# Two layers' attention over one key/value cache: small work, pieces and weights re-timed around the change of layer

## Chip, cores and metric

The kernel runs on one core of one Trainium2 chip. The metric is the device time of one execution in microseconds (us). Engines are named as in the profile: PE (matrix products), DVE (vector work), ACT (activations), POOL, and SP, whose queue issues nearly all DMA transfers.

## What is computed

Two rounds of the same pair of blocks, with one query row per batch, 32 query heads on 8 cache heads, 32768 cached rows of 128 numbers, 2 batches, float32. The shapes that matter: `k_cache` and `v_cache` are (2, 8, 32768, 128), some 537 MB each, and both layers read the same caches and the same weights.

```python
def _A_ref(x, k_cache, v_cache, wq, wo):          # x: (2, 1, 512)
    q = heads(x @ wq)                              # 32 heads of 128
    scores = q . k * (128 ** -0.5)                 # 4 query heads share a cache head
    o = softmax(scores) . v
    return o @ wo                                  # (2, 1, 512)
def _B_ref(x, w1, b1, w2, b2):                     # mixer over one token, 1792 hidden
    h = _layernorm(x)
    return sum_f(_gelu(h * w1 + b1) * w2) + b2
x = x + _A_ref(_layernorm(x), ...)
x = x + _B_ref(_layernorm(x), ...)
x = x + _A_ref(_layernorm(x), ...)
x = x + _B_ref(_layernorm(x), ...)
```

The second layer's query of a batch needs the first layer's whole result for that batch, mixer included.

## The kernel before

**Units and steps.** A unit is (layer, batch, head). Its K and its V are 64 cells each; a cell is 128 partitions x 512 float32, 0.262 MB. `Order` (L41 to L110) writes the sequence by hand as steps of 4 cells (`STEP`): 16 K steps (`k_step`, L328, products at L335), later 16 V steps (`v_step`, L379, products at L388). In the ordinary part K of one unit alternates with V of the unit before. Between K and V of a unit lie its maximum (`max_1`, `max_2`), the transposes (L365) and the exponentials on ACT (L370).

**The two changes of layer** (`changes`, L65). For batch 0, x = (0,0,7) is the last unit of layer 0, y = (1,0,7) the first of layer 1, and fill = (0,1,6) a unit of the other batch put between; for batch 1 they are (0,1,7), (1,1,7) and (1,0,6). x and y use the same cache head, so the first 10 cells of K (`KEPT_K`) and all 64 of V (`KEPT_V`) stay in memory from x to y and are not loaded again. The order is K(x), [V before], K(fill), V(x), V(fill), K(y), V(y) and so on. While the 16 steps of V(fill) run, the mixer of the batch is worked through in hooks after them: hidden tiles on ACT (L527), their products (L511), then `change_0` to `change_3` (L565 to L594), which make the new layer's query row by row. K(y) starts in the step after V(fill).

**Hooks.** `at(p, f, ...)` puts small work behind step p in program order (L705 to L803). Each engine runs its own instructions in that order, so a small product stands in PE's queue between two steps. For a unit these are among others `denominators` (L407: a sum on DVE, a small product L411, a reciprocal L413), `take_out` (L417: the accumulator copied to the tile `row`, of which there is one), `out_1` (products L427, then L442) and `out_2` (products with the output weights, L451). The `us=` of a hook is what the planner is told of its cost. `unread` (L599) issues products whose result nobody reads, on PE alone; one of width G is a product of 512 columns (two PE records, L605).

**Memory and loads.** `mem` holds 106 cells. `plan_loads` (L113) lays out, ahead of time, every transfer: it goes through the steps in order, chooses for each run of missing cells a size (of `SIZES`, 32 down to 4 cells, or the size that `order.sizes` fixes by `cut`, L97) and a place with the least forecast wait, and the step after which the transfer may be issued, that is, after which the last user of that place is done. All these transfers go out in this one order on SP's queue (L823, weights L816); an issue that has to wait for PE holds all later ones. While y's K streams, 64 cells hold the kept V and 16 the weights of heads 6 and 7, which both layers share; 26 are left, 10 of them with the kept K until those steps are done.

**Sizes around the change.** V(fill) goes in 16 pieces of 4 cells. Of K(y), cells 10 and 11 come as one piece of 2; the rest is left to the planner, which made pieces of 4 up to cell 39 and then 8, 8, 8 for the first change, and pieces of 4 up to cell 47 and then 8, 8 for the second.

**Weights.** wq and wo of a head are one transfer of 8 cells. It is asked for 24 steps ahead of the head's first K step (L737), and the query products (`make_q`, L284; products L300) stand 10, 8 and 6 steps ahead of it (L732). Six weights belong to layer 1 alone (heads 5 to 0); that of head 5 comes right behind K of the second y.

Of the kernel before, what the change touches and what calls it, by code (L numbers as in the profile page):

```python
# [14 lines left out]
G = 512  # L15
HALF = 32
STEP = 4
# [4 lines left out]
KEPT_K = 10  # L22
# [18 lines left out]
class Order:  # L41


    def __init__(self, heads):
        far, f, s = list(range(heads - 2)), heads - 2, heads - 1
        self.steps = []
        self.pairs = []
        before = [(0, b, h) for h in far for b in (0, 1)] + [(0, 0, f)]
        x0, fill0, y0 = (0, 0, s), (0, 1, f), (1, 0, s)
        x1, fill1, y1, n = (0, 1, s), (1, 0, f), (1, 1, s), (1, 1, f)  # L50
        after = [(1, b, h) for h in far[:1:-1] for b in (0, 1)] + [(1, b, h) for b in (0, 1) for h in far[1::-1]]
        for i, u in enumerate(before):
            self.k(u)
            if i:
                self.v(before[i - 1])
        self.k(x0), self.v(before[-1]), self.k(fill0), self.v(x0), self.v(fill0)
        self.k(y0), self.v(y0), self.k(x1), self.k(fill1), self.v(x1), self.v(fill1)
        self.k(y1), self.v(y1), self.k(n)
        prev = n
        for u in after:  # L60
            self.k(u), self.v(prev)
            prev = u
        self.v(prev)
        self.last = prev
        self.changes = ((x0, fill0, y0), (x1, fill1, y1))  # L65
        self.units = before + [x0, fill0, y0, x1, fill1, y1, n] + after
        self.first, self.end = {}, {}
        for p, (kind, u, g) in enumerate(self.steps):
            self.first.setdefault((kind, u), p)
            self.end[kind, u, g // HALF] = p  # L70
        byv = sorted(self.units, key=lambda u: self.first["V", u])
        self.v_before = {u: byv[i - 1] if i else None for i, u in enumerate(byv)}
        self.last_of = {
            (layer, b): max((u for u in self.units if u[:2] == (layer, b)), key=lambda u: self.end["V", u, 1])
            for layer in (0, 1)
            for b in (0, 1)
        }
        self.first_of = {
            (layer, b): min((u for u in self.units if u[:2] == (layer, b)), key=lambda u: self.end["V", u, 1])
            for layer in (0, 1)  # L80
            for b in (0, 1)
        }
        self.kept = {}
        for x, _, y in self.changes:
            for g in range(KEPT_K):
                self.kept["K", x, g] = ("K", y, g)
            for g in range(KEPT_V):
                self.kept["V", x, g] = ("V", y, g)
        self.sizes = {}
        for x, fill, y in self.changes:  # L90
            self.cut("K", y, KEPT_K, (-KEPT_K % STEP,))
            self.cut("V", x, HALF, TAPER)
            self.cut("V", fill, 0, (STEP,) * 16)
        self.cut("V", self.last, 0, (HALF // 2, HALF // 2))
        self.cut("V", self.last, HALF, FINAL)
# [100 lines left out]
def gqa_mixer_kernel(ctx: ExitStack, tc: tile.TileContext, x, kt, v, wqo, cols, out):  # L196
# [10 lines left out]
    order = Order(HKV)  # L207
    steps, first, end = order.steps, order.first, order.end
# [498 lines left out]
    def at(p, f, *args, us=0.0):  # L707
        hooks.setdefault(p, []).append((f, args))
        busy[p] = busy.get(p, 0.0) + us
# [6 lines left out]
    changed = {y: (x, fill) for x, fill, y in order.changes}  # L716
    opening = order.units[0]
    weights, made = [], {opening}
    users = {}
    for u in order.units:  # L720
        layer, b, h = u
        users.setdefault(h if h >= HKV - 2 else (layer, h), []).append(u)
        k0 = first["K", u]
# [3 lines left out]
        us = (u, mate) if b == 0 and mate not in made and (layer == 0 or h < HKV - 2) else (u,)  # L727
# [5 lines left out]
    for name, us in users.items():  # L733
        k0 = min(first["K", u] for u in us)
        h = name if isinstance(name, int) else name[1]
        layer = min(u[0] for u in us)
        weights.append((k0 - 24 if k0 else -1, (layer, h), max(end["V", u, 1] for u in us) + 3))  # L737

    for u in order.units:
        layer, b, h = u  # L740
        key = (layer, b)
        k_mid, k_end = end["K", u, 0], end["K", u, 1]
        v0, v_mid, v_end = first["V", u], end["V", u, 0], end["V", u, 1]
        ahead = order.v_before[u]
        p1, p2 = (k_end + 2, k_end + 4) if k_end + 4 < v0 else (k_end, k_end)
        t0 = max(k_mid, end["V", ahead, 0] if ahead else 0)
        t1 = max(k_end, end["V", ahead, 1] if ahead else 0)
        if p2 <= t0:
            at(p1, max_1, u, us=0.2), at(p2, max_2, u, us=0.2)
            at(t0, turn_scores, u, 0), at(t0, exponentials, u, 0)  # L750
        else:
            at(t0, turn_scores, u, 0)
            at(p1, max_1, u, us=0.2), at(p2, max_2, u, us=0.2)
            at(p2, exponentials, u, 0, us=5.0 if p1 == p2 else 0.0)
        at(t1, turn_scores, u, 1)
        at(max(t1, p2), exponentials, u, 1)
        at(v0 - 1 if u == order.last else v_mid + 2, denominators, u, us=0.4)
        if u == order.last:
            at(v0 - 1, take_rows, key)
            at(v0 - 1, table, AF.Gelu_apprx_tanh)  # L760
            at(v0 - 1, mix_1, key)
            at(v0 - 1, last_rows, u)
            at(v_mid, unread, u, G, 3)
            at(v_mid + 4, unread, u, P, 2)
            at(v_end - 2, take_out, u)
            at(v_end - 2, unread, u, G)
            at(v_end - 1, out_sum, u)
            at(v_end, last_mixer, u)
            continue
        at(v_end, take_out, u)  # L770
        if u != order.last_of[key]:
            late = 0 if u == order.v_before[order.last] else 1
            at(v_end + late, out_1, u, us=1.2)
            at(v_end + 2 * late, out_2, u, us=2.0)
            continue
        e = v_end
        at(e - 2, mix_1, key, us=1.2)
        at(e, out_1, u, us=1.9)
        at(e + 1, out_2, u, us=2.0)
        at(e + 1, take_rows, key)  # L780
        at(e + 2, mix_2, key, us=1.2)
        if layer == 0:
            at(e + 2, unread, u, G // 2)
            at(e + 3, half_way, key, us=1.0)
            at(e + 3, unread, u, G)
        at(e + 2, table, AF.Gelu_apprx_tanh)
        for k in range(FT // 2 + 1):
            at(e + 3 + k, hidden_tiles, key, k, us=0.7 if k else 0.0)
        e += 3 + FT // 2
        at(e, take_rows, key)  # L790
        at(e, table, AF.Exp)
        if layer == 1:
            at(e + 1, mix_4, key, us=1.2)
            continue
        (y,) = [y for y, (x, _) in changed.items() if x == u]
        at(e + 1, change_0, key, us=1.0)
        at(e + 1, unread, u, G // 2)
        at(e + 2, change_1, key, y, us=1.2)
        at(e + 3, change_2, key, y, us=0.4)
        at(e + 3, unread, u, G)  # L800
        at(e + 4, change_3, y, us=1.0)
        at(e + 4, unread, u, G // 2)
        assert e + 4 < first["K", y]  # L803

    loads = plan_loads(order, weights, busy)
    finals = [a for label, s, a, _ in loads if label[:2] == ("V", order.last)]
# [83 lines left out]
```

## Time and profile before

| what | value |
|---|---|
| median of 3 runs | 2507.3 us (2506.25 to 2511.06) |
| the profiled execution's own time | 2505.95 us |
| its span in the profile, first to last instruction | 2504.1 us |
| mean granted PE clock | 0.757 of full |
| bytes that SP's queue moved | 1064.32 MB |

The view by windows, which the prediction quotes, gives, for stretches of the span (start:end in us, then the length), the busy time of each engine with its number of instructions, the granted PE clock (1.00 is full, 0.50 half), the mean busy share of the 16 DMA engines, and the GB/s moved. A row of the timeline gives the start and duration, the engine and line, what is read and written, the number of instructions merged, and in brackets how long the engine stood idle before and what ended that.

### The profile page before, as it was taken

To read this page: it belongs to the slowest core of one execution; us is meant where nothing else is said; L and a number is where in the kernel's file an instruction comes from. 1 tells how busy PE (TensorE), PEld (TensorE's weight loads), DVE (VectorE), ACT (ScalarE), POOL (GpSimd) and SP (SyncE) were. 2 spreads that over 40 slices of the span, in tenths; PEclk is the share of its full clock that TensorE was granted. 3 is DMA by queue.
4 is the path that set the end of the run, shared out by engine and by line. 5 is a ranking of instruction groups with operands and counts; after the bars stand their busy time and mean duration, and the time that the engine had idled before them with its cause. 6 is when DMAs were issued, how large, how long until landed. Compare 5 with 4: busy or idle time off the path is not lost. (4 is left out here: it accounts for less than half of the span.)

```text
span 2504.1 us, 21186 instructions
## 1 busy us (share of the span) xinstructions
PE 1383.1 (55%) x9682; PEld 395.9 (16%) x9682; DVE 180.3 (7%) x487; ACT 185.8 (7%) x579; POOL 5.1 (0%) x18
## 2 busy tenths in 40 slices
PE   3455555554455554556776774455465545555567
PEld 1111111111111111111121121111111111111112
DVE  1000000000000000001010010000000000000012
ACT  0100000000000000001110101000000000000021
POOL 0000000000000000000000000000000000000000
PEclk9777776777767767778788887777777777677788
DMA  9999999999999999999999999999999999999996
GB/s 418 431 428 433 436 429 434 436 430 431 432 433 434 433 433 430 416 431 420 409 423 426 414 415 442 432 429 434 431 435 434 429 429 438 429 433 434 428 432 284
DMA packets 33075, 1065.70 MB, mean 426 GB/s; under 512 B 3925, under 2 KB 3929, under 8 KB 5082
## 3 DMA queue, kind: packets, MB, share of 16 engines
q1 hardware_dynamic: 32696, 1064.32, 99.0%
q8 instruction: 76, 1.25, 0.2%
q14 instruction: 13, 0.11, 0.0%
q10 hardware_dynamic: 290, 0.03, 0.0%
HBM read 1064.33 MB, written 0.00 MB: 425 GB/s over the span
## 5 line engine op out<-in xcount | busy, mean ns | idle before, releaser
L335 PE MATMUL scores<-mem,qz 128*32 128x512 f32 x4096 | 605.3, 734 | 549.5 <-DMA mem<-in_kt_dram 549.5
L388 PE MATMUL acc<-mem,S 128*16 128x512 f32 x4080 | 593.2, 714 | 539.7 <-DMA mem<-in_v_dram 534.7
L370 ACT ACTIVATE S<-S,neg 128x128 f32<-128x128 f32 x256 | 129.7, 509 | 2240.9 <-DVE S L365 1205.6
L335 PEld LDWEIGHTS scores<-mem,qz 128*32 128x32 f32 x4096 | 136.4, 128 | 951.1 <-issue 476.2
L388 PEld LDWEIGHTS acc<-mem,S 128*16 128x16 f32 x4080 | 125.1, 107 | 857.2 <-issue 776.6
L345 DVE TENSOR_REDUCE mx<-scores 128x1 f32<-128x512 f32 x64 | 44.2, 691 | 839.5 <-PE scores L335 831.7
L427 PEld LDWEIGHTS misc<-selg,row 128*128 128x128 f32 x256 | 48.9, 285 | 48.2 <-issue 36.8
L365 DVE STREAM_TRANSPOSE S<-scores 128x512 f32<-128x512 f32 x64 | 45.4, 710 | 118.9 <-PE acc L388 118.9
L427 PE MATMUL misc<-selg,row 128*128 128x4 f32 x256 | 51.7, 325 | 3.3 <-DVE row L419 3.2
L451 PE MATMUL rows<-mem,oT 128*1 128x512 f32 x248 | 51.0, 912 | 0.3 <-DVE oT L442 0.3
L370 ACT ACTIVATION_READ_ACCUMULATOR S<-S,neg 128x1 f32 x256 | 47.7, 186 | 0.0
L355 DVE TENSOR_REDUCE m<-misc 1x4 f32<-1x128 f32 x32 | 8.9, 279 | 357.7 <-PE misc L353 357.7
L419 DVE COPY row<-acc 128x512 f32<-128x512 f32 x32 | 22.1, 691 | 173.5 <-PE acc L388 173.5
L413 DVE RECIPROCAL rl<-misc 128x4 f32<-128x4 f32 x32 | 5.8, 182 | 343.3 <-PE misc L411 343.3
L442 DVE TENSOR_TENSOR oT<-misc,rl 128x4 f32<-128x4 f32 x32 | 5.2, 162 | 273.1 <-PE misc L427 272.6
L411 PEld LDWEIGHTS misc<-both,one 128*128 128x128 f32 x64 | 14.1, 275 | 51.7 <-issue 45.7
L300 PE MATMUL misc<-mem,xw 128*32 128x512 f32 x144 | 20.9, 641 | 1.9 <-DVE xw L276 1.9
L307 PEld LDWEIGHTS misc<-selg,row 128*128 128x128 f32 x128 | 16.3, 199 | 17.7 <-issue 8.4
L411 PE MATMUL misc<-both,one 128*128 128x4 f32 x64 | 16.8, 333 | 4.1 <-DVE both L410 4.1
L527 ACT ACTIVATE row<-bcast,bias,scale 128x512 f32<-128x512 f32 x21 | 16.3, 777 | 29.8 <-PE rows L511 16.2
L307 PE MATMUL misc<-selg,row 128*128 128x2 f32 (+1 forms) x128 | 17.7, 260 | 0.8 <-DVE row L292 0.8
L353 PE MATMUL misc<-ident,mxa 128*1 128x128 f32 x64 | 16.7, 354 | 2.1 <-DVE mxa L351 2.1
(119 smaller groups left out, 246.0 us busy)
## 6 DMA issues: line engine op xcount, KB each, us to landing
mem<-in_kt_dram SPq DMA_DIRECT2D x23, 2048.0 KB, 14.0
mem<-in_v_dram SPq DMA_DIRECT2D x37, 1024.0 KB, 8.8
mem<-in_v_dram SPq DMA_DIRECT2D x9, 4096.0 KB, 24.3
mem<-in_wqo_dram SPq DMA_DIRECT2D x14, 2048.0 KB, 33.4
mem<-in_v_dram SPq DMA_DIRECT2D x4, 6144.0 KB, 23.0
mem<-in_kt_dram SPq DMA_DIRECT2D x6, 4096.0 KB, 28.9
mem<-in_kt_dram SPq DMA_DIRECT2D x20, 1024.0 KB, 9.4
mem<-in_v_dram SPq DMA_DIRECT2D x7, 2048.0 KB, 18.0
```

Source lines behind the costliest of these rows:

```text
L300: nc.tensor.matmul(q_ps[us][32 * d : 32 * d + 32, :], xw[:, d, :], wq[:, d, :], start=True, stop=True)
L307: nc.tensor.matmul(pt[:, r * n : (r + 1) * n], q_row[us][:, r * DH : (r + 1) * DH], side, start=True, stop=True,)
L335: nc.tensor.matmul(sc_ps[u, half][32 * row : 32 * row + 32, :], qz[:, at : at + 32], cells(at_cell["K", u, g], 1), start=(i == 0), stop=(i ...
L345: nc.vector.tensor_reduce(mx[u][:, half : half + 1], sc_ps[u, half], axis=AX.X, op=ALU.max)
L353: nc.tensor.matmul(pm[:1, :P], mxa, ident, start=True, stop=True)
L365: nc.vector.transpose(S[half], sc_ps[u, half])
L370: nc.scalar.activation(s[:, :, h], s[:, :, h], AF.Exp, bias=neg[u][:, h : h + 1], scale=SCALE, accum_out=lsum[u][:, half, h : h + 1],)
L388: nc.tensor.matmul(acc[32 * row : 32 * row + R * QT, :], S[half][:, col : col + R * QT], vc, start=(g < NG), stop=(g >= quads - NG),)
L411: nc.tensor.matmul(pl[:, :R], ones, both, start=True, stop=True)
L419: nc.vector.tensor_copy(asb[u], acc)
L427: nc.tensor.matmul(po_of[u][:, :R], asb[u][:, t * DH : (t + 1) * DH], selg[:, t * R : (t + 1) * R], start=(t == 0), stop=(t == QT - 1 and ...
L451: nc.tensor.matmul(rows[b][32 * r : 32 * r + 1, :], oT[u][:, r : r + 1], wo_of(u)[:, r, :], start=(u == order.first_of[layer, b]), stop=(u ...
```

## The change

- `Order`: after the 2 cells that complete the kept 10 to a step, the whole rest of K(y), 52 cells, is cut into 13 pieces of 4.
- Weights of layer 1 are asked for 14 steps ahead of the head's first K step instead of 24.
- A filling unit's `denominators` move from behind the 10th of its V steps (`v_mid + 2`) to behind the 5th (`v0 + 4`). Its `out_1` moves from 1 step behind its V end to 7, its `out_2` from 2 to 9. Both so stand behind K steps of y: the 7th and the 9th, where they stood behind the 1st and the 2nd.
- Behind the 8th to the 15th of the 16 K steps of y stands an `unread` of width G.

```diff
         for x, fill, y in self.changes:
-            self.cut("K", y, KEPT_K, (-KEPT_K % STEP,))
+            self.cut("K", y, KEPT_K, (-KEPT_K % STEP,) + (STEP,) * ((2 * HALF - KEPT_K) // STEP))
...
-        weights.append((k0 - 24 if k0 else -1, (layer, h), max(end["V", u, 1] for u in us) + 3))
+        weights.append((k0 - (24 if layer == 0 else 14) if k0 else -1, (layer, h), max(end["V", u, 1] for u in us) + 3))
...
-        at(v0 - 1 if u == order.last else v_mid + 2, denominators, u, us=0.4)
+        fills = [y for y, (_, fill) in changed.items() if fill == u]
+        at(v0 - 1 if u == order.last else v0 + 4 if fills else v_mid + 2, denominators, u, us=0.4)
...
-            late = 0 if u == order.v_before[order.last] else 1
+            late = 0 if u == order.v_before[order.last] else 7 if fills else 1
             at(v_end + late, out_1, u, us=1.2)
-            at(v_end + 2 * late, out_2, u, us=2.0)
+            at(v_end + (late + 2 if fills else 2 * late), out_2, u, us=2.0)
...
         at(e + 4, unread, u, G // 2)
         assert e + 4 < first["K", y]
+        for p in range(end["K", y, 0], end["K", y, 1]):
+            at(p, unread, u, G)
```

## The prediction

> **What bounds the kernel now.** I read the page first: the share of DMA, then the GB/s by slices.
>
> ```profile
> span 2504.1 us, 21186 instructions
> PE 1383.1 (55%) x9682; PEld 395.9 (16%) x9682; DVE 180.3 (7%) x487; ACT 185.8 (7%) x579; POOL 5.1 (0%) x18
> GB/s 418 431 428 433 436 429 434 436 430 431 432 433 434 433 433 430 416 431 420 409 423 426 414 415 442 432 429 434 431 435 434 429 429 438 429 433 434 428 432 284
> q1 hardware_dynamic: 32696, 1064.32, 99.0%
> ```
>
> No compute engine is the bound (PE 55%); SP's queue, q1, keeps the 16 DMA engines occupied for 99.0% of the span. So only time in which the transfers run below their rate can be won, and the slices show where: some 432 nearly everywhere, 409 to 426 around the two changes of layer. The view by windows sizes it, first the ordinary parts, then 90 us around each change, then stretches with pieces of one size (4 cells, 4 cells, mostly 8 cells).
>
> ```profile
> 150.00:950.00 800.00, 425.23 (x2860) 119.30 (x2860) 48.07 (x125) 42.21 (x160) 0.00 (x0) 0.72 1.00 432
> 1500.00:2400.00 900.00, 468.80 (x3186) 132.18 (x3186) 54.89 (x144) 54.96 (x198) 0.54 (x1) 0.74 1.00 432
> 1200.00:1290.00 90.00, 72.45 (x522) 20.42 (x512) 10.14 (x32) 6.20 (x19) 0.54 (x1) 0.81 1.00 411
> 1400.00:1490.00 90.00, 66.83 (x475) 17.89 (x478) 9.84 (x31) 4.74 (x17) 0.54 (x1) 0.84 0.99 411
> 1180.00:1200.00 20.00, 14.40 (x134) 4.48 (x128) 2.32 (x8) 12.67 (x22) 0.54 (x1) 1.00 1.02 421
> 1370.00:1400.00 30.00, 23.06 (x202) 8.22 (x202) 4.37 (x14) 15.26 (x26) 0.54 (x1) 1.00 1.01 421
> 1266.00:1290.00 24.00, 24.00 (x222) 7.86 (x210) 3.09 (x7) 0.00 (x0) 0.00 (x0) 1.00 1.01 426
> ```
>
> The whole prize: 90 us at 411 instead of 432 is 90 x (1 - 411/432) = 4.4 us, twice, 8.8 us. Part of it is the price of small pieces (421 for 4 cells, 426 for 8) and stays. The rest lies in a few holes:
>
> ```profile
> 1210.00:1222.00 12.00, 11.36 (x92) 3.96 (x84) 1.65 (x7) 0.00 (x0) 0.54 (x1) 1.00 1.00 393
> 1222.00:1234.00 12.00, 7.38 (x32) 0.76 (x32) 1.31 (x2) 0.00 (x0) 0.00 (x0) 0.62 1.02 431
> 1234.00:1238.00 4.00, 1.93 (x8) 0.20 (x8) 0.00 (x0) 0.00 (x0) 0.00 (x0) 0.50 0.86 303
> 1238.00:1250.00 12.00, 6.70 (x36) 1.30 (x40) 0.00 (x0) 0.00 (x0) 0.00 (x0) 0.64 0.98 414
> 1262.00:1266.00 4.00, 4.00 (x40) 0.96 (x36) 0.00 (x0) 0.00 (x0) 0.00 (x0) 0.95 0.91 334
> 1428.00:1432.00 4.00, 2.91 (x16) 0.40 (x16) 0.00 (x0) 0.00 (x0) 0.00 (x0) 0.50 1.01 387
> 1432.00:1440.00 8.00, 3.73 (x20) 0.59 (x16) 0.00 (x0) 0.00 (x0) 0.00 (x0) 0.71 1.00 391
> 1440.00:1444.00 4.00, 2.72 (x16) 0.40 (x12) 0.00 (x0) 0.00 (x0) 0.00 (x0) 0.50 0.71 213
> 1444.00:1456.00 12.00, 8.23 (x52) 1.77 (x48) 1.91 (x5) 4.14 (x16) 0.00 (x0) 0.74 0.98 417
> ```
>
> The timeline of PE and SP says why. These are the last K steps of the two y, and the first V step of the first y:
>
> ```profile
> 1234.37 1.93 PE L335 MATMUL scores<-mem,qz 128*32 128x512 f32 x8 [0.54 <-DMA mem<-in_kt_dram]
> 1249.52 3.21 PE L335 MATMUL scores<-mem,qz 128*32 128x512 f32 x16 [1.89 <-DMA mem<-in_kt_dram]
> 1252.81 0.69 DVE L345 TENSOR_REDUCE mx<-scores 128x1 f32<-128x512 f32 x1 [20.09 <-PE scores L335]
> 1257.37 11.25 PE L388 MATMUL acc<-mem,S 128*16 128x512 f32 x80 [2.40 <-ACT S L370]
> 1437.66 3.64 PE L335 MATMUL scores<-mem,qz 128*32 128x512 f32 x16 [4.27 <-DMA mem<-in_kt_dram]
> 1441.33 0.33 SPq L816 DMA_DIRECT2D mem<-in_wqo_dram  x1
> ```
>
> A place comes free only when PE has used what lies there. Pieces of 8 cells mean two steps at half clock (3.64 us) before the next transfer may go, and one other piece in flight. In the second change SP waits for just that: the two steps from 1437.66 end at 1441.3, the weights of head 5 are issued at 1441.33, and DMA falls to 213 GB/s. In the first, the step at 1234.37 ends at 1236.3 and DMA is at 303.
>
> **The change, part by part.**
>
> *K of y in pieces of 4.* 26 cells are open beside the kept V and the shared weights, over six pieces of 4. Each is freed by one step, and with pieces of 4 in flight the next place has been free for several pieces when it is wanted; 1410 to 1428 in the second change, where pieces of 4 are still in use, shows no hole. So the holes of the tails go. Against 426 for pieces of 8 and 421 for pieces of 4 the holes are, first change: 4 x (1 - 303/426) = 1.15, 12 x (1 - 414/426) = 0.34, 4 x (1 - 334/426) = 0.86, together 2.35 us; second: 4 x (1 - 387/421) = 0.32, 8 x (1 - 391/426) = 0.66, 4 x (1 - 213/426) = 2.00, 12 x (1 - 417/426) = 0.25, together 3.23 us. I count the hole at 1262 in, as V(y) then starts earlier: one step instead of two follows the last landing (3.21 us before).
>
> ```profile
> 1410.00:1428.00 18.00, 13.27 (x88) 2.88 (x88) 1.47 (x3) 0.00 (x0) 0.00 (x0) 0.76 1.01 421
> 1209.73 0.59 PE L605 MATMUL misc<-ident,one 128*1 128x512 f32 x1
> 1210.15 0.59 PE L605 MATMUL misc<-ident,one 128*1 128x512 f32 x1
> 1277.74 4.47 PE L335 MATMUL scores<-mem,qz 128*32 128x512 f32 x40
> ```
>
> The price: five pieces of 8 (three and two) become ten of 4. 2.097 MB take 4.98 us at 421 and 4.92 at 426, so 0.06 each, 0.3 us in all.
>
> One rule speaks against small pieces. The Trainium skill, page "DMA: Bandwidth & Descriptors", section "Anatomy of one DMA — SWDGE (gpsimd) path", gives each DMA a fixed cost of about 2.0 us beside its bytes; five more pieces would by it cost 10 us, and the sum would come out at 2511.8, no gain at all. The trace disagrees for transfers that queue up: 20 and 30 us of nothing but 1.05 MB pieces ran at 421 GB/s, 2.49 us for each, which leaves no 2 us between them.
>
> *Unread products.* Each is two records 0.42 us apart at full clock, so 0.85 us, about twice that at half. A K step is 1.93 us at half clock; with 1.7 beside it PE needs 3.6 where a piece of 4 comes each 2.49. PE then has no pause, and the row at 1257.37 shows what follows: it begins in a half-clock stretch and from 1262 the clock is 0.95 to 1.00. At full clock a step is 0.9 us (40 records in 4.47), with its product about 1.75 of 2.49. I take PE to be up to 3 us late around the 9th step and level again by the 15th; 26 cells are 16 us of transfers, so that hides. If it does not, see the rivals. Their gain, a K step faster by about 0.9 us, is inside the holes counted above.
>
> *The filling unit's work.* `out_1` and `out_2` stood between the first three K steps, which use kept cells; PE then waited for DMA anyway, so taking them away gains nothing there. At their new place, behind the 7th and 9th step, each is about 1 us at full clock, two at half, DMA pieces being 2.49 apart; it is in the 3 us above. `denominators` leave the chain of the query:
>
> ```profile
> 1201.63 0.15 DVE L410 TENSOR_TENSOR both<-lsum 128x4 f32<-128x4 f32 x1
> 1201.93 0.35 PE L411 MATMUL misc<-both,one 128*128 128x4 f32 x2 [1.04 <-DVE both L410]
> 1216.24 1.05 PE L427 MATMUL misc<-selg,row 128*128 128x4 f32 x8
> 1218.11 1.04 PE L451 MATMUL rows<-mem,oT 128*1 128x512 f32 x8
> ```
>
> That is 0.3 to 0.6 us on PE just before `change_0`. The hole behind this chain, 1210 to 1222, is 12 x (1 - 393/421) = 0.8 us and gets 0.3 back by 1234 (431), net 0.5. I take half, 0.25 us (between 0 and 0.5).
>
> *Weights later.* Bytes and sizes stay. Head 5's weights no longer stand behind K(y), where SP waited for them; pieces of K of the next unit do, and take any place that is free. For the other five the transfer moves from between two K halves to between two V halves of 32 cells, while `make_q` stands behind the 7th of the first half's eight steps. Such a half looks like this; the first two rows belong to one half, the last begins the next.
>
> ```profile
> 1630.10 3.62 PE L388 MATMUL acc<-mem,S 128*16 128x512 f32 x16 [10.80 <-DMA mem<-in_v_dram]
> 1638.88 1.04 PE L300 MATMUL misc<-mem,xw 128*32 128x512 f32 x8
> 1649.44 3.62 PE L388 MATMUL acc<-mem,S 128*16 128x512 f32 x16 [8.66 <-DMA mem<-in_v_dram]
> ```
>
> `make_q` ran 8.8 us after the half had landed; 8 cells land 4.9 us behind it (2.097 MB at 426). So it does not wait. I take 0; the bounds are a hold of PE of 4.9 us, five times, which the 8.66 us that PE then idles hide, and about 1 us in all, either way, by where places come free.
>
> **Sum:** 2.35 + 3.23 + 0.25 - 0.3 = 5.5 us less. The profiled execution took 2505.95 us for a span of 2504.1; it would take 2500.4. The median of the runs is 2507.3, 1.35 above it, and the forecast is made against that: 2501.8. All transfers behind the second change run at their rate, so what is won there arrives at the end.
>
> **Rivals.** *The wait moves to the start of V(y)* (0.20). From the end of K(y) to the first V step lie 4.56 us (1252.81 to 1257.37) that no edit touches; DMA must live on cells that K steps freed. With landing, step, chain, the first V step and the issue that is 8 to 11 us, against some 20 free cells of the 26, 12.4 us at 421 GB/s: it should fit, but by little. If half of both tails comes back as a hole there, 2.8 us are lost again: 2504.6, no change by the bound below.
>
> *The change does not do what it says* (0.08): the planner, told other costs, makes other pieces and places in the stretch after, and new holes eat the old ones. 2507.
>
> *More goes* (0.05): the first chain hole vanishes, and the ordinary half-and-half part profits from weights in V: another 2 us, 2499.8.
>
> *Unread products at half clock* (0.08), the slower case. If the granted clock stays at half through the K tail, each of the eight steps is 3.6 - 2.5 = 1.15 late, 9.2 us at the end. V(y) starts that much later while DMA has 12.4 us of cells for 9.2 and the 9.5 (middle of 8 to 11): a hole of 6.3 in each change, 12.6 us, against 5.8 that go: 2507.3 + 12.6 - 5.5 = 2514.4. It decides itself at the fourth or fifth of these steps; the 1.00 at 1266 to 1290 with PE always busy speaks against it.
>
> *Late weights hold PE* (0.02, slower): five holds of 4.9 us with nothing to hide them would be 24.5, so 2526; that needs a half in which PE has no pause left, and the rows show 8.66 and 10.80. *Each small piece pays a hole of its own* (0.02), the skill's rule as a mechanism of this kernel: five more holes like that at 1234, 1.15 us each, 5.8 us, and the gain is gone: 2507.6.
>
> **The numbers.** The forecast, holes gone, has 0.55, and 0.43 of it lies beyond 5 us. Two runs of this kernel differ by that much, so 0.2%, 5 us, is what a measurement tells from no change. Faster 0.48 (0.43 + 0.05), same 0.42 (0.12 of the forecast, 0.20, 0.08, 0.02), slower 0.10 (0.08 + 0.02). Range 2498.0 to 2508.0: below it is more than the prize of 8.8; above it lie the half-clock case and late weights.
>
> **What would show it.** Right: no window of 4 us under 400 GB/s in the K tails; the last K piece lands some 2 us earlier against the first V(fill) step; one L335 step of 8 records after it; granted clock 1.00 in the second half of K(y). Wrong: DMA share under 0.95 between the end of K(y) and the third V step (the wait moved); L335 records of 1.9 us through to the end of K(y) (half clock); SP waiting on PE for pieces that follow V(y) (other places).

## The result

The changed kernel takes 2512.6 us (median of 16 runs, 2510.0 to 2518.82) against 2507.55 us before (16 runs): ratio 1.0021, 95% interval 1.0015 to 1.0028, so some 5.3 us slower where 5.5 us faster was forecast. The profiled execution has a span of 2511.0 us.

The page of the changed kernel, the rows that answer to those of before:

```profile
span 2511.0 us, 21268 instructions
GB/s 418 433 434 430 432 435 431 433 429 433 434 433 432 433 434 432 410 413 426 401 425 422 407 428 440 432 434 431 419 437 433 422 431 422 427 434 432 431 431 287
q1 hardware_dynamic: 34424, 1064.32, 98.8%
```

The same bytes, in more packets. The dips around the two changes of layer are still there, and new ones stand in the second half (419, 422, 422, 427), where before nearly all slices had 428 to 438. The view by windows of the changed kernel, 90 us around each change and 600 us of the ordinary second layer:

```profile
1200.00:1290.00 90.00, 73.37 (x522) 20.60 (x511) 9.72 (x29) 7.67 (x21) 0.54 (x1) 0.89 0.99 404
1400.00:1490.00 90.00, 71.66 (x516) 21.40 (x512) 10.02 (x32) 4.74 (x17) 0.54 (x1) 0.91 1.00 415
1700.00:2300.00 600.00, 309.93 (x2094) 87.68 (x2094) 36.13 (x95) 31.66 (x120) 0.00 (x0) 0.73 1.00 429
```

and the last of these for the kernel before:

```profile
1700.00:2300.00 600.00, 314.73 (x2136) 88.85 (x2140) 35.45 (x94) 31.66 (x120) 0.00 (x0) 0.73 1.00 432
```

404 and 415 where there were 411 and 411: the prize at the changes was not taken. 429 for 432 over 600 us is 600 x (1 - 429/432) = 4.2 us, lost where I had expected nothing.

The two spans can't be compared directly. Some 2 us of their difference arose before 1180 us, where the two programs are the same, and nearly all of that between 1060 and 1120 us:

```profile
1060.00:1120.00 60.00, 31.30 (x206) 8.58 (x202) 3.70 (x10) 4.22 (x16) 0.00 (x0) 0.73 0.98 418
1060.00:1120.00 60.00, 29.13 (x197) 7.83 (x189) 3.54 (x9) 4.22 (x16) 0.00 (x0) 0.70 0.96 405
```

The first row is the kernel before, the second the changed one. What is lost there is not the change's, and it differs between executions; only the ratio of the runs counts.

**Where the second layer loses.** Two of the new dips, by windows, and behind them the first stretch in the kernel before:

```profile
1786.00:1794.00 8.00, 5.31 (x29) 1.65 (x33) 0.28 (x1) 0.00 (x0) 0.00 (x0) 0.50 0.93 367
1950.00:1956.00 6.00, 5.73 (x34) 1.66 (x34) 0.28 (x1) 0.00 (x0) 0.00 (x0) 0.58 0.91 352
1786.00:1794.00 8.00, 2.87 (x16) 0.69 (x17) 0.00 (x0) 0.00 (x0) 0.00 (x0) 0.50 1.00 434
```

and the timeline of the first, PE and SP:

```profile
1788.69 3.61 PE L388 MATMUL acc<-mem,S 128*16 128x512 f32 x16 [9.98 <-DMA mem<-in_v_dram]
1790.65 0.33 SPq L826 DMA_DIRECT2D mem<-in_v_dram  x1
```

At 1788.69 the first V half of head 4 has landed; its 16 records are two steps at half clock, 1.8 us each. At 1790.65, right behind the first step, SP issues the second half. In the list of transfers that the program makes, the first half lies in cells 74 to 105 and the second in 46 to 77: they share four cells, and those are the first step's. Before, the two halves had cells 74 to 105 and 42 to 73. With the weights between the halves, the planner's forecast said that the first step would be done in time, so the shared place counted as free, and of the places without a forecast wait it takes the highest. Four V halves of layer 1 got such a place (heads 4, 3 and 2 of batch 0, head 2 of batch 1). (A window counts a DMA packet where it starts, so windows of a few us scatter widely, up to 456 GB/s next to such a hole; the dips are to be read together with the rows of SP and the 600 us.)

**Where the K tails lose.** The forecast holes of before are replaced by others. The first two rows are the changed kernel, the last two the kernel before:

```profile
1230.00:1236.00 6.00, 6.00 (x29) 2.33 (x32) 1.48 (x3) 0.00 (x0) 0.00 (x0) 0.60 0.77 284
1425.00:1431.00 6.00, 6.00 (x33) 2.49 (x34) 1.48 (x3) 0.00 (x0) 0.00 (x0) 0.64 0.85 318
1230.00:1236.00 6.00, 4.90 (x24) 0.40 (x16) 1.31 (x2) 0.00 (x0) 0.00 (x0) 0.50 1.00 427
1425.00:1431.00 6.00, 4.80 (x24) 0.40 (x16) 0.00 (x0) 0.00 (x0) 0.00 (x0) 0.50 1.02 401
```

Against 421 that is 6 x (1 - 284/421) = 2.0 and 6 x (1 - 318/421) = 1.5 us. The timeline of the first:

```profile
1227.62 1.94 PE L335 MATMUL scores<-mem,qz 128*32 128x512 f32 x8 [0.55 <-DMA mem<-in_kt_dram]
1229.49 1.87 PE L427 MATMUL misc<-selg,row 128*128 128x4 f32 x8
1231.29 1.94 PE L335 MATMUL scores<-mem,qz 128*32 128x512 f32 x8
1233.29 2.91 SPq L826 DMA_DIRECT2D mem<-in_kt_dram  x3
```

The 7th step, then `out_1` at half clock (1.87 us), then the 8th step, and only then, at 1233.29, SP issues cells 40 to 43 of K. They were given the place of cells 28 to 31, with only two transfers between the two, although 26 cells were open. Three pieces of each K tail stand like that: 40, 52 and 60. I call a transfer tight whose place is freed by a step that waits for data with no more than 8 cells, some 5 us of transfers, queued between those data and the transfer. The number of transfers alone does not say it: in the ordinary part most halves of 32 cells take a place whose last data landed two or three transfers ahead, but there 32 cells or more lie between.

### The profile page after: what moved, and what is told of

Read it like the earlier page. It is cut to its first block, busy times and chain, and to the rows that moved or that the text cites. A ratio compares the mean times of both kernels' runs of the same rounds, so it can differ in the third digit from the quotient of the medians.

```text
span 2511.0 us, 21268 instructions
## 1 busy us (share of the span) xinstructions
PE 1398.3 (56%) x9714; PEld 401.1 (16%) x9714; DVE 180.3 (7%) x487; ACT 185.8 (7%) x579; POOL 5.1 (0%) x18
## 5 line engine op out<-in xcount | busy, mean ns | idle before, releaser
L605 PE MATMUL misc<-ident,one 128*1 128x512 f32 (+1 forms) x52 | 25.5, 574 | 0.0
```

Of the source, the lines that this page charges most:

```text
L605: nc.tensor.matmul(idle[0][:1, :n], one, S[0][:, :n] if u == order.last else ident[:, :1].to_broadcast([P, n]), start=True, stop=True)
```

## The experiments

Two theories. **Places**: the loss sits at tight transfers, because the planner's forecast of when a place is free is too early (`LEAD_US` 1.5 and 1.6 us for a step), and it prefers a high place to one long free. **Crowding**: the unread products and the filling unit's work beside y's K steps hold PE up. A third, for the second layer: later weights cost by themselves. All ratios are to the kernel before, measured beside it in 5 rounds.

**Weights back** (changed kernel):

```diff
-        weights.append((k0 - (24 if layer == 0 else 14) if k0 else -1, ...
+        weights.append((k0 - 24 if k0 else -1, ...
```

> The changed kernel with all weights asked for 24 steps ahead again. Two theories. Places: the loss sits where a transfer was given cells whose last user's data land only one or two transfers earlier, so that SP waits for PE and DMA runs dry; four such V halves of 32 cells (layer 1, heads 4, 3, 2 of batch 0 and head 2 of batch 1) came with the later weights and are gone here, the tight pieces in the K tails stay. It expects 3 to 4 us less than the changed kernel, ratio to before 1.0005 to 1.001, and 432 GB/s from 1700 to 2200. Crowding: the loss comes from the unread products and the filling unit's work beside y's K steps, which stay: ratio 1.002.

2507.88 us, 1.0005 (0.9996 to 1.0013). Windows:

```profile
1700.00:2300.00 600.00, 312.27 (x2128) 88.58 (x2132) 35.49 (x94) 31.65 (x120) 0.00 (x0) 0.73 1.00 432
```

Some 4 us of the loss go with the four tight V halves; the rest of the change, forecast to win 5.5 us, then shows no gain (the interval reaches from 1.0 us faster to 3.3 us slower), and the two stretches of 90 us stand at 412 and 414 GB/s.

**No unread products** (changed kernel without its last two lines).

> The changed kernel without the unread products behind y's K steps, with the very same list of transfers. Places expects a small gain, 0 to 2 us (PE frees the tight pieces of the K tails some tenths sooner each), ratio 1.0015 to 1.002. Crowding expects 4 to 6 us less than the changed kernel, ratio 0.9995 to 1.0005.

2512.66 us, 1.0022 (1.0012 to 1.0032): no difference. Crowding by them is out. The hole in the first K tail is shallower than in the changed kernel, that in the second about as deep:

```profile
1230.00:1236.00 6.00, 5.47 (x28) 0.89 (x24) 1.31 (x2) 0.00 (x0) 0.00 (x0) 0.50 0.97 373
1425.00:1431.00 6.00, 6.00 (x30) 1.40 (x33) 1.47 (x3) 0.00 (x0) 0.00 (x0) 0.51 0.87 330
```

**A longer lead in the planner** (changed kernel, all its edits):

```diff
-LEAD_US = 1.5
+LEAD_US = 4.0
```

> The changed kernel with one constant of the planner raised, LEAD_US from 1.5 to 4.0, so that a place counts as free without a wait only if its last user is done 4 us ahead of the queue; all edits of the change stay. No transfer then takes a place just landed in, at the price of some more pieces (75 of 4 cells for 69). Places expects the loss gone and the forecast gain of the change to show: ratio 0.997 to 0.9995. Crowding expects no more than 1 us from it: ratio 1.0015 to 1.002.

2503.76 us, 0.9986 (0.9977 to 0.9994). One constant turns the change from slower to faster. The holes in the K tails are gone:

```profile
1230.00:1236.00 6.00, 6.00 (x36) 1.30 (x29) 0.61 (x1) 0.00 (x0) 0.00 (x0) 0.72 1.01 423
1425.00:1431.00 6.00, 6.00 (x39) 1.59 (x38) 0.00 (x0) 0.00 (x0) 0.00 (x0) 1.00 1.02 423
1200.00:1290.00 90.00, 74.24 (x540) 20.99 (x536) 11.24 (x33) 5.48 (x19) 0.54 (x1) 0.92 1.01 422
1400.00:1490.00 90.00, 73.33 (x518) 20.82 (x520) 10.33 (x29) 4.14 (x16) 0.54 (x1) 0.90 1.02 429
1060.00:1120.00 60.00, 35.43 (x242) 9.83 (x238) 3.71 (x10) 4.22 (x16) 0.00 (x0) 0.72 1.01 434
```

The last row shows that the constant does more than mend the change: it also closes holes between 1060 and 1120 us, ahead of the change, which the kernel before has too. That is 60 x (1 - 418/434) = 2.2 us of the gain. All four runs with lead 4.0 throughout have 433 to 435 in this stretch, all others 405 to 419. So the runs further down, with the longer lead for some transfers only, are the cleaner evidence.

**Later weights alone** (kernel before, that one line of the change).

> The kernel before with the later weights alone. Its V halves behind the weights happen to get other cells (74 to 105) that were freed long before; only one half of 32 (V of the first unit behind the second change) is tight. Places expects little, 0 to 2 us more: ratio 1.000 to 1.0008. If later weights cost by themselves, because they stand between two V halves, it is the 3.7 us that the changed kernel lost behind 1530 us: ratio 1.0015.

2511.15 us, 1.0015 (1.0007 to 1.0024). The number is that of the rival, and my expectation of 0 to 2 us is missed. The place is not the rival's:

```profile
1454.00:1462.00 8.00, 8.00 (x64) 1.97 (x68) 0.00 (x0) 1.98 (x8) 0.00 (x0) 0.82 0.66 252
1700.00:2300.00 600.00, 314.29 (x2130) 88.40 (x2122) 36.14 (x95) 31.65 (x120) 0.00 (x0) 0.73 1.00 433
```

The second layer runs at 433 with the weights between V halves, so they cost nothing there. 8 x (1 - 252/426) = 3.3 us go in one hole, and the timeline shows what for:

```profile
1449.12 0.33 SPq L816 DMA_DIRECT2D mem<-in_wqo_dram  x1
1454.00 7.64 PE L388 MATMUL acc<-mem,S 128*16 128x512 f32 x56 [2.40 <-ACT S L370]
1458.28 3.49 SPq L823 DMA_DIRECT2D mem<-in_kt_dram  x3
```

Behind the weights of head 5 the next K piece was given a place that the third step of V(y) frees; V(y) starts at 1454.00, so SP issues it at 1458.28, 9 us after the weights. Moving one request re-dealt the places, and one piece got a place that comes free too late. It is not tight in the sense above, as the kept V landed long before: it waits for the chain between K(y) and the start of V(y).

**Lead for the V halves only** (changed kernel; `wait` reckoned with 4.0 where the transfer is a second V half of layer 1, the last unit left out).

> The changed kernel with the planner's lead raised to 4.0 only for second V halves of layer 1; the weights stay late. The four V halves behind late weights then take cells that were freed a whole half earlier. Three tight pieces in the first K tail stay, and the second stretch gets five others. Places expects the steady part (1700 to 2300) back at 432 GB/s and a ratio of 1.0002 to 1.0012. If lateness of the weights by itself costs, the steady part stays at 427 and the ratio at 1.002.

2507.96 us, 1.0002 (0.9993 to 1.0011). Late weights stay, their loss is gone:

```profile
1700.00:2300.00 600.00, 320.22 (x2132) 89.88 (x2136) 35.48 (x94) 31.65 (x120) 0.00 (x0) 0.73 1.00 432
```

**Lead for y's K pieces only** (changed kernel):

```diff
-                    wait = max(0.0, t + LEAD_US - queue)
+                    wait = max(0.0, t + (4.0 if label[0] == "K" and label[1] in [y for _, _, y in order.changes] else LEAD_US) - queue)
```

> The changed kernel with the planner's lead raised to 4.0 only for the K pieces of the two y; everything else of the change stays, late weights and unread products included. The list then has no tight piece from 1100 us to the tail (the V halves behind the weights fall on other cells by themselves). Places expects a ratio of 0.998 to 0.9995, near the run with lead 4.0 everywhere (0.9986). If the pieces, the unread products or the late weights cost by themselves, it stays over 1.0005.

2504.21 us, 0.9987 (0.9978 to 0.9996). The unread products, the filling unit's work beside y's K steps and the late weights are all still in, so none of them costs the 5 us.

```profile
1200.00:1290.00 90.00, 72.61 (x532) 20.27 (x525) 9.90 (x30) 5.83 (x19) 0.54 (x1) 0.92 1.02 426
1400.00:1490.00 90.00, 69.80 (x506) 18.92 (x504) 10.40 (x29) 4.14 (x16) 0.54 (x1) 0.94 1.01 425
1700.00:2300.00 600.00, 315.29 (x2144) 88.93 (x2144) 36.80 (x96) 32.93 (x125) 0.00 (x0) 0.74 1.00 431
```

**Three V halves made tight again** (the kernel of the run above; their place is written by hand). One of the three came out as 24 + 8 cells.

```diff
             spots = range(CELLS - s + 1)
+            if label in (("V", (1, 0, 3), HALF), ("V", (1, 0, 2), HALF), ("V", (1, 1, 2), HALF)):
+                spots = [next(l[2] for l in loads[::-1] if l[0] == ("V", label[1], 0)) - s + STEP]
```

> The run with lead 4.0 for y's K pieces alone (0.9987), and in it three second V halves of layer 1 (heads 3 and 2 of batch 0, head 2 of batch 1) forced into a place that overlaps the first half of the same V by one step, as the changed kernel had it. Nothing else is meant to differ. Places expects 2 to 3.5 us more than that run: ratio 0.9995 to 1.0003, with DMA dipping where these halves begin (near 1950, 2110 and 2195 us). If places don't matter, 0.9987 again.

2507.91 us, 1.0001 (0.9992 to 1.0010): 0.0014 or 3.5 us for three tight halves, at the upper end of what was expected (the two intervals just overlap). The holes are where they were put, and the stretch falls from 431 to 428:

```profile
1942.00:1950.00 8.00, 5.97 (x40) 1.86 (x44) 0.39 (x2) 0.00 (x0) 0.00 (x0) 0.66 0.92 363
2105.00:2111.00 6.00, 4.55 (x25) 1.31 (x29) 0.28 (x1) 0.00 (x0) 0.00 (x0) 0.50 1.04 396
2190.00:2196.00 6.00, 5.16 (x29) 1.54 (x33) 0.28 (x1) 0.00 (x0) 0.00 (x0) 0.50 0.93 347
1700.00:2300.00 600.00, 313.75 (x2112) 88.11 (x2116) 35.50 (x94) 31.66 (x120) 0.00 (x0) 0.72 0.99 428
```

**Single edits.** Pieces of 4 alone (kernel before, the `cut` line of the change):

> The kernel before with K of y in pieces of 4 alone. One tight piece is left in each K tail, the last one, in place of four pieces of 8. Places expects most of the forecast gain: ratio 0.9982 to 0.9995. If small pieces cost by themselves (a fixed price for each transfer), it is 1.000 to 1.003.

2505.45 us, 0.9992 (0.9983 to 1.0000): 2 us won, with the 90 us around the changes at

```profile
1200.00:1290.00 90.00, 69.31 (x518) 19.33 (x522) 10.14 (x32) 6.72 (x20) 0.54 (x1) 0.87 1.01 421
1400.00:1490.00 90.00, 69.77 (x493) 18.53 (x496) 9.87 (x31) 4.51 (x17) 0.54 (x1) 0.82 1.01 423
```

The filling unit's work moved alone (kernel before, the three lines with `fills`):

> The kernel before with the filling unit's work moved alone, and so with other costs told to the planner. Its list gets tighter in the second K tail: a piece of 16 cells at the 11th step, and head 5's weights wait for a step whose data land in the transfer right before. Places expects a loss, 1 to 5 us: ratio 1.0003 to 1.002. By the blind forecast (chain 0.25 us shorter, out products into slack) it is 0.9998 to 1.0000.

2507.81 us, 1.0003 (0.9995 to 1.0012). The interval holds both expectations, so the time can't tell. The stretches do not follow the list: the second, whose list got tighter, stands at 413, and the first, whose list holds no tight piece, fell from 411 to 405. Its deepest hole is at the start of V(y), 281 GB/s from 1266 to 1270 us; why it is deeper there is not shown.

```profile
1200.00:1290.00 90.00, 68.35 (x502) 19.07 (x495) 9.73 (x29) 7.67 (x21) 0.54 (x1) 0.85 0.99 405
1400.00:1490.00 90.00, 70.85 (x520) 20.87 (x512) 10.03 (x32) 4.75 (x17) 0.54 (x1) 0.84 0.99 413
```

The longer lead alone (kernel before):

> The kernel before with the planner's lead at 4.0 alone, K of y not cut. The weights of head 5 stay very tight behind the second K, the rest of the list has room. Places expects part of the gain: ratio 0.9985 to 0.9998. If pieces of 4 are what the run with both gained by, 1.000.

2505.72 us, 0.9995 (0.9986 to 1.0004). The first change is healed, the second, where head 5's weights wait for the 15th K step, is worse than before:

```profile
1200.00:1290.00 90.00, 69.34 (x526) 20.09 (x522) 10.47 (x33) 5.39 (x19) 0.54 (x1) 0.89 1.01 424
1400.00:1490.00 90.00, 67.22 (x470) 17.82 (x472) 8.82 (x25) 4.14 (x16) 0.54 (x1) 0.82 0.96 404
```

**All edits and lead 4.0, no unread products.**

> All edits of the change with lead 4.0 (0.9986) but without the unread products, with the same list of transfers. If the products help (K steps at full clock), ratio 0.999 to 0.9995; if they cost, 0.997 to 0.998; places by itself expects no difference, 0.998 to 0.999.

2504.82 us, 0.9987 (0.9978 to 0.9996), against 0.9986 with them: they neither help nor cost.

**Pieces of 4 and lead 4.0 alone** (kernel before, two lines):

> The kernel before with K of y in pieces of 4 and the planner's lead at 4.0: no unread products, the filling unit's work and the weights where they were. Against the run with all edits and lead 4.0 (0.9986) it says what those edits give when no place is tight. Places expects the same within its interval, 0.998 to 0.9995; if the unread products and the moved work are what fills the holes, 0.9995 to 1.001.

2502.26 us, 0.9978 (0.9969 to 0.9987), the fastest of all and a little under the range expected: 5.5 us below before by the ratio, and some 10 below the changed kernel.

```profile
1200.00:1290.00 90.00, 73.04 (x522) 19.59 (x522) 11.49 (x35) 5.19 (x19) 0.54 (x1) 0.85 1.01 423
1400.00:1490.00 90.00, 71.05 (x508) 18.61 (x504) 11.04 (x33) 4.27 (x17) 0.54 (x1) 0.83 1.01 420
1700.00:2300.00 600.00, 317.56 (x2140) 88.73 (x2132) 36.80 (x96) 32.39 (x123) 0.00 (x0) 0.75 1.00 433
```

Its interval overlaps that of all edits with lead 4.0, so whether the other three edits cost something is open; they do not gain.

## Why the prediction was wrong

*K of y in pieces of 4: the step that failed.* The holes were read and sized about rightly, and pieces of 4 do close them where the list leaves room: alone they lift the two stretches from 411 and 411 to 421 and 423, which is 90 x (1 - 411/421) + 90 x (1 - 411/423) = 4.7 us, where the sum had 2.35 + 3.23 - 0.3 = 5.3. That the fastest run is 5.5 us below before, the very sum, is partly luck: with the longer lead some 2 us of its gain lie between 1060 and 1120 us, ahead of all that was changed in the pieces. The sentence that failed is "with pieces of 4 in flight the next place has been free for several pieces when it is wanted". It holds for a ring that takes the oldest free place. The planner takes the highest place that its forecast calls free, and with other costs told to it and other sizes it put three pieces of each tail where data had just landed. With the pieces alone only one of each tail is tight; with the filling unit's work moved as well, and its cost told to the planner at other steps, there are three. The times, 0.9992 and 1.0005, point the same way, though their intervals overlap. The list follows from code that was in hand; I reasoned about how many cells were open and not about which one is taken. In place of -5.6 us for the two tails came no gain clear of noise: about +1.2, between -1.0 and +3.3 (weights back, 1.0005, all else in place).

*Weights later: mis-sized.* "I take 0 ... about 1 us in all, either way, by where places come free". The mechanism was named; it measured 4 us (1.0021 against 1.0005), as four tight halves and not as late weights: the products of `make_q` did not wait for DMA in the changed kernel, and with the V halves elsewhere the second layer runs at 432 with late weights too.

*The rival* that the planner "makes other pieces and places in the stretch after, and new holes eat the old ones" is what happened. It got 0.08 and a price of zero net; the holes were larger than the old ones and lay also 300 to 700 us behind the change.

*Unread products: right that they hide.* The clock did rise in the K tail, as the row at 1257.37 let expect; in the changed kernel a K step is 1.9 us at 1231.29 and 1.1 here:

```profile
1243.97 1.06 PE L335 MATMUL scores<-mem,qz 128*32 128x512 f32 x8 [0.99 <-DMA mem<-in_kt_dram]
1253.95 1.07 PE L335 MATMUL scores<-mem,qz 128*32 128x512 f32 x8 [2.96 <-DMA mem<-in_kt_dram]
1260.05 11.47 PE L388 MATMUL acc<-mem,S 128*16 128x512 f32 x80 [2.40 <-ACT S L370]
```

So the half-clock rival fell. But faster K steps won nothing either way (1.0022, and 0.9987 against 0.9986): DMA sets the pace there.

*The filling unit's work: not shown to gain.* `out_1` at half clock took the 1.9 us that I had given it, but it stood just ahead of the step that a tight piece waited for, so it was not in slack. What it cost of the 2.0 us hole wasn't separated. The 0.25 us for `denominators` are not borne out either: the rate from 1210 to 1222 does not follow their place. With them moved it is 419 in the changed kernel but 396 with weights back and 385 with this work alone; left where they were it is 393 before but 421 with the pieces alone.

*The price of small pieces: small, as forecast.* By the fixed cost that the prediction cites from the Trainium skill (page "DMA: Bandwidth & Descriptors", section "Anatomy of one DMA — SWDGE (gpsimd) path"), five more transfers would cost 10 us. Here the transfers queue up on SP's queue: the run with pieces alone, five transfers more, is 2 us faster than before, and with lead 4.0 5.5 us, with 75 pieces of 4 cells for 57. The 0.3 us itself is too small for these runs.

*The start of V(y)*, the first rival, came in part. The chain from the end of K(y) to V(y) takes 4.96 us in the changed kernel (1255.09 to 1260.05), against 4.56. The hole behind it, 0.86 us of the sum, was to go; it stayed and moved with V(y):

```profile
1266.00:1270.00 4.00, 4.00 (x40) 0.96 (x36) 0.00 (x0) 0.00 (x0) 0.00 (x0) 1.00 0.84 305
```

That is 4 x (1 - 305/426) = 1.1 us, and SP waits there for the products of V(y). In the runs with pieces of 4 and lead 4.0 no such hole shows (422 and 423 over the 90 us of the first change).

## What to carry to other kernels

Where a planner deals out memory ahead of time, an edit to any size, cost or request re-deals all that follows. Before pricing the edit, read off the new list, for each transfer, how long before its turn its place is freed, and by which step; the shortest of these are the holes. A forecast that is a microsecond or two too early is paid at each of them, and a margin in the planner can be worth more than the re-timing it was meant to serve.

## What was not expected of the hardware

A transfer of 8.4 MB, issued at 1790.65 while weights of 2.1 MB were still under way ahead of it, came too late, though it seemed early enough. PE could begin on the half before at 1788.69, the weights take 4.9 us, so the queue should have lasted to about 1793.6, 2.9 us behind the issue. Yet DMA fell to 367 GB/s in those 8 us.

The single packets in the changed kernel's trace show why. The 16 DMA engines did not finish these transfers together: they ended their shares of the half between 1784.46 and 1788.09, and each went straight on to its share of the weights, 4.9 us for most. So they ran out of work one by one, the first at 1789.36, the last at 1792.97. The first packet of the new half starts at 1791.61, 0.96 us after the issue; ten of the 16 engines were without work by then.

```profile
1788.70:1789.40 0.70, 0.70 (x4) 0.14 (x8) 0.00 (x0) 0.00 (x0) 0.00 (x0) 0.50 0.99 421
1789.40:1791.60 2.20, 2.20 (x16) 0.51 (x9) 0.00 (x0) 0.00 (x0) 0.00 (x0) 0.50 0.56 238
```

PE's start shows the last of the 16 engines, and the first ran out of work 3.6 us ahead of the last; here the issue had to beat the first. A lead of 4.0 us in the planner was enough wherever it had a place to give; with the longer lead alone, the weights of head 5 still had to wait for the 15th K step, and the second change stayed at 404.
